# A chunked mLSTM with a gated network behind it: q and k transposed by TensorE in four tiles and scored in fp32, in place of scaled halves and DMA transposes

## The chip, the cores and the metric

The kernel runs on one core of a Trainium2 chip. The metric is the device time of one execution in microseconds (us). TensorE (PE) multiplies matrices, VectorE (DVE), ScalarE (ACT) and GpSimd (POOL) work on elements, SyncE (SP) issues most DMAs. PE's clock is granted in shares of full speed; the profile shows the share.

## The reference

Inputs: q, k, v and the output gate o, each (4 batches, 8 heads, 768 tokens, 40), two scalar gates per head and token, and three matrices of a network.

```
for t in range(S):
    m_new = np.maximum(f_gate[:, :, t] + m, i_gate[:, :, t])
    f_stab = np.exp(f_gate[:, :, t] + m - m_new)
    i_stab = np.exp(i_gate[:, :, t] - m_new)
    m = m_new
    C = f_stab * C + i_stab * einsum('bhd,bhe->bhde', vt, kt)
    n = f_stab * n + i_stab * kt
    h_tilde = einsum('bhde,bhe->bhd', C, qt)
    denom = np.maximum(np.abs(einsum('bhd,bhd->bh', n, qt)), 1.0)
    y[:, :, t] = sigmoid(o_gate[:, :, t]) * h_tilde / denom
# y as x (4, 768, 320):
gate = sigmoid(causal depthwise convolution of x with 5 taps)
return (gate * (x @ w_val)) @ w_out
```

All of it is fp32; the three matrices of the network come as 64-bit numbers, which the kernel turns into fp32 itself.

## The kernel before, in words

**Tiling.** The 768 tokens are cut into 6 steps `j` of 128 tokens, each step into two chunks `p` of 64. A unit of work `u = 4 j + b` is a step and a batch: a pair of chunks, 8 heads each. A chunk is numbered `g = 2 u + p`, 48 in all. Inside a chunk the recurrence is written as attention: a matrix of 128 rows (64 keys of the chunk and, on the other 64 rows, the state carried in, of which 40 or 41 are used) by 64 queries, per head.

**The steps of a chunk.** `args` (L357): one bf16 matmul gives the exponents' arguments of 8 heads, psd; `expo` (L368, ACT) takes their exponential, dm. `scores` (L384) gives k times q for the keys and q itself for the state rows, pss. `probs` (L391, DVE) multiplies the two, pt. `keyw` (L403, POOL) weights the keys, kw. `heads` (L437, L439) is written by hand, alternating for each head a matmul of the output, ph, into one half of PE's columns with one of the new state, pc, into the other. `state_out` (L419, ACT) copies the state into the values' tile vc of the next chunk. For each pair follow `norm` (L448 to L452, DVE), `norm_o` (L457, POOL), `gate_o` (L462, DVE) and a transpose of the result, px (L471), whose copies feed the network.

**How scores are made.** q and k are loaded in their natural layout, tokens on partitions, into nat. For each batch the largest absolute value of a token is taken (`prep_max`, L288, ACT), a power of two is made of it by integer arithmetic (`prep_scale`, L293 to L300, DVE), and the scaled values are split into two fp16 halves and a copy of the first (`prep_hi`, L322, POOL; `prep_lo`, L327 and L336, DVE), side by side in a tile stk of 128 by 8 heads by 128. A DMA transpose of the whole tile (`prep_tr`, L347, SP) gives tq or tk with the 120 used columns on partitions; an fp16 matmul over these 120 sums the products of the halves. `probs` takes the scale of k out again, and the norm uses the scale of q, which is brought into the tokens' order by small matmuls (L309, L315, L316). A second set of DMAs copies k from nat into kp (L197), the natural layout with the state rows that `keyw` needs.

**The network.** Each step's 128 tokens of the four batches go through it about a step later: `conv0`, `conv` and `conv3` (L496, L502, L514), sigmoid (L522), `val` (L537, pf), products and their split into two parts (L542 to L551), `outp` (L563, po), stored by L568 and L572. The last step runs in two halves of two batches. In the first third, the matrices are loaded and converted on DVE, POOL and ACT (L581 to L623).

**Order.** Start-up is written out by hand. Behind it, every step is put on a list with a time in chunks (the table LAGS gives a lag for each step, some for single `j`), the list is sorted, and a scheduler orders each engine's instructions from that; SP keeps the list's order. Inside the marked blocks PE keeps the written order of its instructions, though others may come between. The psd, pss, px, pg, pf and po tiles share five PSUM buffers, ph has two, pc one.

Of the kernel before, what the change touches and what calls it, by code (L numbers as in the profile page):

```python
# [8 lines left out]
F32 = mybir.dt.float32  # L9
# [79 lines left out]
def tile_mlstm_gated_ffn(  # L89
# [26 lines left out]
    SB = 14  # L116
# [4 lines left out]
    R = B  # L121
    PB = P // B
# [32 lines left out]
    nat = [cst.tile([P, 2, BH, D], F32, name=f"nat{i}") for i in range(2)]  # L155
    kp = cst.tile([P, 2, BH, D], F32, name="kp")
# [16 lines left out]
    tk_ = [cst.tile([P, L + H * (P + L)], F16, name=f"tk{i}") for i in range(3)]  # L173
    cmp_ = [cst.tile([P, 2, B], F32, name=f"cmp{i}") for i in range(2)]
    sct = [cst.tile([P, B], F32, name=f"sct{i}") for i in range(2)]
    spg = cst.tile([P, PB, R], BF16, name="spg")
    sel_g = cst.tile([P, PB], F32, name="sel_g")
    sel_b = cst.tile([P, B], BF16, name="sel_b")
    scl = [cst.tile([P, 2, B], F32, name=f"scl{i}") for i in range(2)]
    amx = [cst.tile([P, 2, B], F32, name=f"amx{i}") for i in range(2)]  # L180
    stk = [cst.tile([P, 2, H, P], F16, name=f"stk{i}") for i in range(2)]


    def load_qk(j, x, b0, b1):
        ts = slice(j * P, (j + 1) * P)
        if x == 1 or j == 0:
            hs = slice(b0 * H, b1 * H)
            nc.sync.dma_start(nat[j % 2][:, x, hs], (qv, kv)[x][ts, hs])
            return
        dst = nat[j % 2][:, 0].rearrange("p (h r) d -> p h (r d)", r=R)  # L190
        for b in range(b0, b1):
            nc.sync.dma_start(dst[b * PB : (b + 1) * PB], q[b, :, ts].rearrange("h (g r) d -> g h (r d)", r=R))

    def load_k(j, p, i):
        hs = slice(i * BH // 2, (i + 1) * BH // 2)
        put = nc.scalar.copy if j == i == 0 else nc.vector.tensor_copy if j < T["kpe"] else nc.sync.dma_start
        put(kp[TOK[p] : TOK[p] + L, p, hs], nat[j % 2][p * L : (p + 1) * L, 1, hs])  # L197
# [80 lines left out]
    MASKE = 0x7F800000  # L278

    def part(j, x, i):  # L280
        src = nat[j % 2][:, x]
        if x == 0 and j > 0:
            return src.rearrange("p (h r) d -> p h r d", r=R)[:, :, i]
        return src[:, i * H : (i + 1) * H]

    def prep_max(j, i, x):
        junk = wk.tile([P, H, D], BF16, name=f"junk{j}_{i}_{x}", tag="junk", bufs=1)
        nc.scalar.activation(junk, part(j, x, i), AF.Abs, accum_out=amx[j % 2][:, x, i : i + 1])  # L288

    def prep_scale(j, xs, i0, i1):  # L290
        a, s = (t[j % 2][:, xs, i0:i1] for t in (amx, scl))
        c = cmp_[j % 2]
        nc.vector.tensor_scalar_max(a, a, 2.0**-100)  # L293
        nc.vector.tensor_scalar(a.bitcast(I32), a.bitcast(I32), MASKE, None, op0=ALU.bitwise_and)
        nc.vector.tensor_scalar(
            s.bitcast(I32), a.bitcast(I32), -1.0, float((SB + 254) << 23), op0=ALU.mult, op1=ALU.add
        )
        for p in range(2 if xs.stop == 2 else 0):
            h = slice(TOK[p], TOK[p] + L)
            nc.vector.tensor_scalar(  # L300
                c.bitcast(I32)[h, p, i0:i1],
                amx[j % 2].bitcast(I32)[p * L : (p + 1) * L, 1, i0:i1],
                float(-(SB << 23)),
                None,
                op0=ALU.add,
            )
# [626 lines left out]
```

## Time and profile before

| | |
|---|---|
| median of 3 runs | 294.26 us (293.21 to 295.13) |
| the profiled execution's own time | 294.18 us |
| its span, first to last instruction | 292.4 us |
| mean granted PE clock | 0.837 |
| busy PE, DVE, ACT, POOL | 207.6, 227.9, 155.4, 176.7 us |
| DMA: bytes, packets | 38.73 MB, 145897 |

Busy time of PE is the union of its matmuls, whose ends are modelled and which overlap in its pipeline; how fast matmuls follow each other is read from their starts, or from the chain of waits, in which a piece lasts until the next begins. A slice of the page is 7.3 us.

### The profile page before, as it was taken

The numbers are of one execution on the slowest core, as the hardware profiler recorded it, in microseconds if no ns is written. First come the engines' busy times: TensorE is split into PE (matmuls) and PEld (weight loads), VectorE is DVE, ScalarE is ACT, GpSimd is POOL, SyncE is SP. The second block draws the span as 40 slices with busy tenths as digits, with TensorE's granted clock in tenths as the row PEclk, the third lists the DMA queues.
The fourth block names the chain that finished last, engine by engine and source line by source line (L and its number), as shares of the span: only waits on it lengthen the run. The fifth ranks groups of instructions, "written<-read, shape, count | busy, mean of one in ns | idle before, by whom it ended". The sixth has DMA issues, their size and how long they took to land.

```text
span 292.4 us, 6704 instructions
## 1 busy us (share of the span) xinstructions
PE 207.6 (71%) x2411; PEld 165.9 (57%) x2411; DVE 227.9 (78%) x526; ACT 155.4 (53%) x354; POOL 176.7 (60%) x276
## 2 busy tenths in 40 slices
PE   0037437526649374798479989876989999999985
PEld 0015325325437263575468666765767877787984
DVE  7999968757588999988999756997539992794950
ACT  4276642373774932578552497822288456346262
POOL 7566426533749844978964655783439762855541
PEclk9999755556855776789759999795799999999999
DMA  7899799999999995399953999975999230011112
GB/s 138 150 148 197 105 204 162 189 153 163 186 174 230 203 143 106 57 190 206 155 85 74 110 214 192 193 67 96 192 225 150 84 83 2 0 45 48 45 47 90
DMA packets 145897, 38.73 MB, mean 132 GB/s; under 512 B 135176, under 2 KB 143752, under 8 KB 145864
## 3 DMA queue, kind: packets, MB, share of 16 engines
q1 hardware_dynamic: 143044, 37.76, 79.0%
q10 hardware_dynamic: 2820, 0.54, 1.3%
q8 instruction: 19, 0.31, 0.5%
q14 instruction: 14, 0.11, 0.1%
HBM read 17.87 MB, written 4.23 MB: 76 GB/s over the span
## 4 chain that ended last, share of the span: by engine, by line
DVE 24%; PE 22%; POOL 14%; DMA 14%; issue 13%; ACT 6%; SPq 5%; ACTq 0%; POOLq 0%; DVEq 0%
DVE sg L502 6%; PE po L563 5%; PE ph L437 5%; PE pf L537 4%; DMA tq<-stk 4%; DMA tk<-stk 3%; DVE stk L327 3%; POOL kw L403 3%; DVE stk L336 3%; DMA sg<-in_o_gate_dram 2%; PE pss L384 2%; PE pg L514 2%; DMA kp<-nat 2%; DVE pt L391 2%; POOL xl L487 2%
## 5 line engine op out<-in xcount | busy, mean ns | idle before, releaser
L437 PE MATMUL ph<-vc,pt 128*64 128x41 f32 (+1 forms) x768 | 69.8, 258 | 28.6 <-ACT vc L419 17.3
L437 PEld LDWEIGHTS ph<-vc,pt 128*64 128x64 f32 (+1 forms) x768 | 61.9, 167 | 41.0 <-ACT vc L419 20.0
L322 POOL TENSOR_SCALAR stk<-nat,scl 128x320 f16<-128x320 f32 x48 | 32.9, 689 | 40.5 <-DMA tk<-stk 17.9
L502 DVE SCALAR_TENSOR_TENSOR sg<-xc,cwt,sg 128x512 f32<-128x512 f32 (+1 forms) x56 | 50.6, 934 | 4.1 <-POOL sg L496 4.0
L439 PE MATMUL pc<-vc,kw 128*40 128x41 f32 (+1 forms) x704 | 51.5, 236 | 3.1 <-POOL kw L403 1.8
L384 PE MATMUL pss<-tq,tk 120*128 120x64 f16 x384 | 35.5, 270 | 21.5 <-DMA tq<-stk 6.4
L439 PEld LDWEIGHTS pc<-vc,kw 128*40 128x40 f32 (+1 forms) x704 | 45.8, 137 | 7.1 <-issue 3.1
L384 PEld LDWEIGHTS <-tk 120*128 120x128 f16 x384 | 28.8, 134 | 34.5 <-issue 19.0
L368 ACT ACTIVATE dm<-psd 128x512 f32<-128x512 f32 x48 | 28.6, 597 | 32.0 <-DVE pt L391 19.9
L403 POOL TENSOR_TENSOR kw<-kp,dm 128x320 f32<-128x320 f32 (+1 forms) x44 | 37.3, 850 | 9.2 <-DMA kp<-nat 3.1
L391 DVE SCALAR_TENSOR_TENSOR pt<-pss,cmp,dm 128x512 f32<-128x512 f32 x48 | 35.6, 741 | 8.0 <-PE ph L437 6.4
L357 PE MATMUL psd<-ra,la 120*128 120x512 bf16 x48 | 23.7, 494 | 23.8 <-DMA la<-gda 18.4
L327 DVE SCALAR_TENSOR_TENSOR stk<-nat,scl,stk 128x320 f16<-128x320 f32 x48 | 31.7, 660 | 10.7 <-POOL stk L322 10.6
L288 ACT ACTIVATE junk<-nat 128x320 bf16<-128x320 f32 x48 | 22.5, 470 | 22.6 <-DMA nat<-in_q_dram 11.6
L457 POOL TENSOR_TENSOR rs<-sg,den 128x320 f32<-128x320 f32 x24 | 19.4, 807 | 22.4 <-DVE den L452 12.0
L419 ACT COPY vc<-pc 40x328 f32<-40x328 f32 x44 | 18.7, 425 | 24.8 <-PE ph L437 17.7
L487 POOL TENSOR_TENSOR xl<-xc,xh 128x256 fp32r<-128x256 f32 x24 | 19.9, 829 | 16.2 <-ACT xc L480 16.0
L542 DVE TENSOR_TENSOR sg<-pf,sg 128x512 f32<-128x512 f32 (+3 forms) x21 | 12.6, 609 | 13.7 <-ACT sg L522 6.5
L551 POOL TENSOR_TENSOR zl<-sg,zh 128x512 fp32r<-128x512 f32 (+1 forms) x14 | 16.1, 1156 | 11.1 <-ACT zh L546 11.0
L336 DVE COPY stk<-stk 128x320 f16<-128x320 f16 x48 | 21.3, 445 | 0.0
L563 PE MATMUL po<-woh,zh 128*128 128x320 f32 x72 | 19.8, 332 | 0.0
L563 PE MATMUL po<-wol,zh 128*128 128x320 f32 x72 | 18.7, 312 | 0.0
(150 smaller groups left out, 443.4 us busy)
## 6 DMA issues: line engine op xcount, KB each, us to landing
nat<-in_q_dram SPq DMA_DIRECT2D x24, 160.0 KB, 4.0
vc<-in_v_dram SPq DMA_DIRECT2D x12, 320.0 KB, 5.6
sg<-in_o_gate_dram SPq DMA_DIRECT2D x6, 640.0 KB, 6.6
out_dram<-ob SPq DMA_DIRECT2D x24, 160.0 KB, 2.4
kp<-nat SPq DMA_DIRECT2D x22, 160.0 KB, 3.5
nat<-in_k_dram SPq DMA_DIRECT2D x10, 320.0 KB, 4.7
nat<-in_k_dram SPq DMA_DIRECT2D x4, 160.0 KB, 3.5
rawv<-in_moe_w_val_dram SPq DMA_DIRECT2D x4, 160.0 KB, 3.2
```

Of the source, the lines that this page charges most:

```text
L322: return nc.gpsimd.tensor_scalar(o, v, f, 1.0, op0=ALU.mult, op1=ALU.mult)
L327: nc.vector.scalar_tensor_tensor(t[:, :, lo : lo + D], part(j, x, i), scl[j % 2][:, x, i : i + 1], t[:, :, 0:D], op0=ALU.mult, op1=ALU.sub ...
L336: return put(t[:, :, dup : dup + D], t[:, :, 0:D])
L368: nc.scalar.activation(dm, psd_[g], AF.Exp)
L384: nc.tensor.matmul(o, tk[h], tq[:, h], start=True, stop=True)
L391: nc.vector.scalar_tensor_tensor(pt, pss_[g], cmp_[j % 2][:, p, b : b + 1], dmt[g], op0=ALU.mult, op1=ALU.mult)
L403: (nc.vector if turn("on_dve_kw", b) else nc.gpsimd).tensor_mul(kw[0:n], kp[0:n, p, b * H : (b + 1) * H], dmt[g][0:n, :, L - 1 : L].to_bro ...
L437: nc.tensor.matmul(pht[u][p * L : (p + 1) * L, h], ptt[g][0:n, h], mv, start=True, stop=True)
L439: nc.tensor.matmul(pc[n0 : n0 + D, h], kwt[g][0:n, h], mv, start=True, stop=True)
L487: (nc.vector if turn("on_dve_xl", b) else nc.gpsimd).tensor_sub(xlb[j % 2][:, :, b], xb[:, :, b, 4:], xhb[j % 2].bitcast(F32)[:, :, b])
L502: nc.vector.scalar_tensor_tensor(o, xc[j % 2][:, c, b0:b1, t : t + P], cwt[:, c, t : t + 1], o, op0=ALU.mult, op1=ALU.add)
L563: nc.tensor.matmul(pf, z, w, start=(i == 0), stop=(i == len(mm) - 1))
```

## The change

q and k are no longer scaled, split and transposed by DMA. k is loaded straight from DRAM into kp, which now has two buffers, and q into nat, which holds q alone. For each pair `tr` (L276 of the changed kernel) transposes q and k on TensorE: fp32 matmuls of 64 tokens by 64 or 40 columns against a 64 by 64 identity. Two heads and the two chunks make four tiles of a quarter of the array each: the chunk chooses the row half, the head of a pair the column half. The result is two PSUM tiles pT per pair, one per chunk, with the even heads' 40 columns on the lower partitions and the odd heads' on the upper. `tr_out` (L287) copies them into SBUF, the first on ACT, the second on DVE (in the first step both on ACT). `scores` (L303, L307) then makes both chunks of a pair at once in fp32: 16 matmuls over 40 rows, again in quarter tiles, and 4 of 256 columns that carry q to the state rows through the identity; the results lie in two PSUM tiles pss, one for even and one for odd heads. `probs` (L337) becomes two multiplications per chunk, without a scale. The norm uses the constant 1. pT and pss come from the same five PSUM buffers as before. The scaling steps, their constants and the q scale's small matmuls are gone. Start-up is written anew: the first four pairs are transposed there, the first pair of chunks is scored there, the constants for the other steps are copied there, and the second spread of the gates goes out on SP. The table LAGS is as before; the transposes of a pair stand 4.7 chunks ahead of it, the loads of a step 11.6 and 7.6 chunks ahead. The copies of the identity into kp, four now, moved from ACT to POOL.

```
-    nat = [cst.tile([P, 2, BH, D], F32, name=f"nat{i}") for i in range(2)]
-    kp = cst.tile([P, 2, BH, D], F32, name="kp")
+    nat = [cst.tile([P, BH, D], F32, name=f"nat{i}") for i in range(2)]
+    kp = [cst.tile([P, 2, BH, D], F32, name=f"kp{i}") for i in range(2)]
...
+    def load_k(j, p, b0, b1):
+        hs = slice(b0 * H, b1 * H)
+        c = slice(j * P + p * L, j * P + (p + 1) * L)
+        nc.sync.dma_start(kp[j % 2][TOK[p] : TOK[p] + L, p, hs], kv[c, hs])
...
-    def prep_hi(j, i, x):
...
-        return nc.gpsimd.tensor_scalar(o, v, f, 1.0, op0=ALU.mult, op1=ALU.mult)
...
-        nc.sync.dma_start_transpose(t, stk[i % 2][:, x].rearrange("p h n -> p (h n)"))
...
+    def tr(u):
+        j, b = divmod(u, B)
+        pT = [ps_s.tile([P, 2, H // 2, L], F32, name=f"pT{u}_{r}", tag="big") for r in range(2)]
+        kf = kp[j % 2].rearrange("p x n d -> p (x n d)")
+        qf = nat[j % 2].rearrange("p n d -> p (n d)")
+        with tc.manual_schedule(engines={mybir.EngineType.PE}):
+            for h in range(0, H, 2):
+                for x in range(2):
+                    for r in range(2):
+                        rows = slice(r * L, (r + 1) * L)
+                        for i, m in ((0, L), (1, D)):
+                            c = (b * H + h + i) * D + (x * (1 - r)) * BH * D
+                            nc.tensor.matmul(
+                                pT[r][i * L : i * L + m, x, h // 2],
+                                (qf, kf)[x][rows, c : c + m],
+                                ident[rows, rows],
+                                start=True,
+                                stop=True,
+                            )
+        qk_ps[u] = pT
+
+    def tr_out(u, r):
+        t = wk.tile([P, 2, H // 2, L], F32, name=f"qk{u}_{r}", tag=f"qk{r}", bufs=4)
+        (nc.scalar.copy if r == 0 or u < B else nc.vector.tensor_copy)(t[0:NT], qk_ps[u][r][0:NT])
+        qk_[u, r] = t
...
+    def scores(u):
+        eo = [ps_s.tile([P, 2, H // 2, L], F32, name=f"pss{u}_{i}", tag="big") for i in range(2)]
+        q = [qk_[u, p][:, 0] for p in range(2)]
+        k = [qk_[u, 1 - p][:, 1] for p in range(2)]
+        rows = [slice(i * L, i * L + D) for i in range(2)]
+
+        with tc.manual_schedule(engines={mybir.EngineType.PE}):
+            for h in range(H // 2):
+                for p in range(2):
+                    for i, r in enumerate(rows):
+                        o = eo[i][TOK[p] : TOK[p] + L, p, h]
+                        nc.tensor.matmul(o, k[p][r, h], q[p][r, h], start=True, stop=True)
+            for p in range(2):
+                for i, r in enumerate(rows):
+                    o = eo[i][STA[p] : STA[p] + L, p]
+                    nc.tensor.matmul(o, ident[r, i * L : (i + 1) * L], q[p][r], start=True, stop=True)
...
-        nc.vector.scalar_tensor_tensor(
-            pt, pss_[g], cmp_[j % 2][:, p, b : b + 1], dmt[g], op0=ALU.mult, op1=ALU.mult
-        )
+        po, do = (t.rearrange("k (h i) l -> k i h l", i=2) for t in (pt, dmt[g]))
+        for i in range(2):
+            nc.vector.tensor_mul(po[:, i], pss_[u][i][:, p], do[:, i])
...
+            at(t - 4.7, tr, u)
+            for r in range(2):
+                at(t - 4.4, tr_out, u, r)
+        if u > 0:
+            at(t + lag("scores", j), scores, u)
```

PE in the kernel before, one pair of the third step, where nothing of the network lies between (names: psd the arguments, tk and tq the transposed halves, pss the scores, ph and pc the heads, px the result's transpose):

```order
L357 MATMUL psd_1457<-ra,la 128x512
L384 LDWEIGHTS tk_100
L384 MATMUL pss_1469<-tq_986,tk_100 128x4x16
...
L437 MATMUL ph_1283<-vc_85,pt_1312 64x41
L439 MATMUL pc_1355<-vc_85,kw_1213 40x41
...
L357 MATMUL psd_1516<-ra,la 128x512
L384 MATMUL pss_1522<-tq_986,tk_100 128x4x16
...
L437 MATMUL ph_1418<-vc_84,pt_1384 64x41
L439 MATMUL pc_1419<-vc_84,kw_1259 40x41
...
L471 MATMUL px_1533<-ident,x_1506 128x128 x2
```

Each chunk has its arguments, its eight scores and its eight heads in turn. PE in the changed kernel, a pair where the second step ends (nat holds q, kp holds k, pT the transposes of one chunk, qk their copies; pss_0 belongs to the even heads, pss_1 to the odd):

```order
L317 MATMUL psd_1545<-ra,la 128x512
L303 MATMUL pss_0_1559<-qk_0_1374,qk_1_1376 64x64
L303 MATMUL pss_1_1560<-qk_0_1374,qk_1_1376 64x64
...
L307 MATMUL pss_0_1559<-qk_0_1374,ident 64x256
...
L381 MATMUL ph_1518<-vc_86,pt_1542 64x41
L383 MATMUL pc_1588<-vc_86,kw_1417 40x41
...
L317 MATMUL psd_1619<-ra,la 128x512
L415 MATMUL px_1634<-ident,x_1609 128x128 x2
L276 MATMUL pT_0_1639<-ident,nat_81 64x64
L276 MATMUL pT_0_1639<-ident,nat_81 40x64
L381 MATMUL ph_1677<-vc_85,pt_1616 64x41
L276 MATMUL pT_1_1640<-ident,nat_81 64x64
```

The scores of both chunks stand together, and 32 transposes of a later pair come in, with the first head of the next pair among them. DVE in the kernel before, in the third step (stk the fp16 halves, pt the probabilities):

```order
L327 SCALAR_TENSOR_TENSOR stk_115<-nat_81,scl_110,stk_115 128x8x40
L336 COPY stk_115<-stk_115 128x8x40
L300 TENSOR_SCALAR cmp_104<-amx_113 64x2
L391 SCALAR_TENSOR_TENSOR pt_1384<-pss_1333,cmp_103,dm_1243 128x512
L327 SCALAR_TENSOR_TENSOR stk_114<-nat_82,scl_111,stk_114 128x8x40
L336 COPY stk_114<-stk_114 128x8x40
```

DVE in the changed kernel, a pair where the second step ends (qk_1 the second transposed tile, den the norm, x the result):

```order
L287 COPY qk_1_1549<-pT_1_1482 104x512
L337 TENSOR_TENSOR pt_1616<-pss_0_1559,dm_1451 128x4x64
L337 TENSOR_TENSOR pt_1616<-pss_1_1560,dm_1451 128x4x64
L392 TENSOR_SCALAR den_1614<-ph_1518 128x8
L337 TENSOR_TENSOR pt_1711<-pss_0_1559,dm_1552 128x4x64
L337 TENSOR_TENSOR pt_1711<-pss_1_1560,dm_1552 128x4x64
L394 TENSOR_TENSOR den_1614<-ph_1518,den_1614 128x8
L396 RECIPROCAL den_1614<-den_1614 128x8
L406 TENSOR_TENSOR x_1944<-ph_1518,rs_1709 128x320
```

The halves, copies and scale arithmetic are gone from DVE; one copy of a transposed tile and two half-size multiplications per chunk stand in their place.

More of the change, by code (lines that the diff above doesn't have):

```diff
@@ L172, in tile_mlstm_gated_ffn, with load_q @@
     cwt = cst.tile([P, 3, 5], F32, name="cwt")
[L173 to L197, printed above, removed]
+    def load_q(j, b0, b1):
+        hs = slice(b0 * H, b1 * H)
+        nc.sync.dma_start(nat[j % 2][:, hs], qv[j * P : (j + 1) * P, hs])
+    def load_k(j, p, b0, b1):
+        hs = slice(b0 * H, b1 * H)
+        c = slice(j * P + p * L, j * P + (p + 1) * L)
+        nc.sync.dma_start(kp[j % 2][TOK[p] : TOK[p] + L, p, hs], kv[c, hs])
     def load_v(j, p):
@@ L275, in spread_in @@
             )
[L278 to L296, printed above, removed]
-        )
[L298 to L306, printed above, removed]
@@ L308, in scale_mul @@
-    def scale_mul(j):
-        nc.vector.tensor_mul(
-            spg, sel_g[:, :, None].to_broadcast([P, PB, R]), scl[j % 2][:, 0, None, :].to_broadcast([P, PB, R])
-        )
-    def scale_out(j):
-        pq = ps_s.tile([P, B], F32, name=f"pq{j}", tag="big")
-        nc.tensor.matmul(pq, spg.rearrange("p g r -> p (g r)"), sel_b, start=True, stop=True)
-        nc.vector.tensor_copy(sct[j % 2], pq)
-    def prep_hi(j, i, x):
-        o, v, f = stk[i % 2][:, x, :, 0:D], part(j, x, i), scl[j % 2][:, x, i : i + 1]
-        if j > 0 and turn("on_act_hi", 2 * i + x):
-            return nc.scalar.activation(o, v, AF.Copy, scale=f)
-        return nc.gpsimd.tensor_scalar(o, v, f, 1.0, op0=ALU.mult, op1=ALU.mult)
@@ L761, in tile_mlstm_gated_ffn @@
-        nc.vector.tensor_copy(sct[0], scl[0][:, 0])
-        run(rest)
-        spread_out(1, nc.scalar.dma_start)
-        for i in range(2):
-            load_qk(1, 1, 2 * i, 2 * i + 2)
-        nc.gpsimd.memset(gt[L:P, 2], 0.0)
-        i4 = ident.rearrange("p (b g) -> p b g", b=B)
-        with nc.allow_low_precision("one of each sum is 1, the others 0"):
-            nc.vector.tensor_reduce(sel_b, i4, axis=AX.X, op=ALU.add)
-        nc.vector.tensor_reduce(sel_g, i4.rearrange("p b g -> p g b"), axis=AX.X, op=ALU.add)
@@ L772, in consts1 @@
-    def consts1():
-        for j in range(1, NJ):
-            yield nc.vector.tensor_copy(ra[:, :, j], tr)
-            yield nc.vector.tensor_copy(la[:, :, j], tl)
+        for g in range(2):
+            args(g)
+        scores(0)
+        for g in range(2):
+            expo(g)
+            keyw(g)
+        for _ in range(6):
+            next(rest)
+        for g in range(2):
+            probs(g)
+        sig_o(0)
+        run(rest)
+        spread_out(1, nc.sync.dma_start)
+        *_, last_dve = consts1()
@@ L777, in consts2 @@
+        load_q(1, 0, B)
+        for p in range(2):
+            load_k(1, p, 0, 2)
+        spread_in(1, nc.sync.dma_start)
+        for p in range(2):
+            load_k(1, p, 2, 4)
     def consts2():
@@ L779, in consts2 @@
             yield vc_const(1, p)
+        for p in range(2):
+            yield kp_const(1, p)
+        nc.gpsimd.memset(gt[L:P, 2], 0.0)
         nc.gpsimd.memset(xc[0][:, :, :, 0:4], 0.0)
```

191 lines of the change are left out of this document (45 added, 146 removed).

## The prediction

> **What bounds the kernel now.** I read the page's busy shares and slices first, then one row per stage, then the chain of waits for prices at full clock.
>
> ```profile
> PE 207.6 (71%) x2411; PEld 165.9 (57%) x2411; DVE 227.9 (78%) x526; ACT 155.4 (53%) x354; POOL 176.7 (60%) x276
> PE   0037437526649374798479989876989999999985
> DVE  7999968757588999988999756997539992794950
> PEclk9999755556855776789759999795799999999999
> DMA  7899799999999995399953999975999230011112
> ```
>
> No engine is full throughout. DVE (VectorE) is nearest; the DMA engines stay at 9 tenths for most of the first 30 slices, while PE (TensorE) gets half its clock in slices 6 to 13. So I cut the span into start-up (A), the first eight pairs of chunks (B, little gated-network work), the other sixteen (C), and the tail behind the last heads (D), by the starts of the heads' matmuls. The columns are PE, weight loads, DVE, ACT (ScalarE) and POOL (GpSimd) busy, then clock, DMA share, GB/s.
>
> ```profile
> 0.00:22.90 22.90, 2.32 (x21) 1.37 (x21) 20.30 (x59) 10.77 (x24) 14.36 (x35) 1.00 0.91 150
> 22.90:115.40 92.50, 50.76 (x694) 39.99 (x694) 76.14 (x195) 47.99 (x116) 53.78 (x88) 0.65 1.10 171
> 115.40:258.30 142.90, 124.87 (x1496) 98.05 (x1496) 112.78 (x238) 81.42 (x180) 94.36 (x136) 0.89 0.76 122
> 258.30:292.40 34.10, 29.62 (x203) 26.51 (x202) 18.70 (x38) 15.21 (x36) 14.16 (x18) 1.00 0.17 59
> 240.00:265.00 25.00, 25.00 (x231) 19.77 (x231) 16.69 (x32) 12.71 (x28) 14.46 (x21) 1.00 0.08 27
> PE pss L384 <- DMA tq<-stk: 6.4, 1, 6.4
> POOL stk L322 <- DMA tk<-stk: 10.4, 6, 3.9
> ```
>
> B is slow, 92.5/8 = 11.6 us a pair, with DMA over-full (1.10), PE at 0.65 clock, and waits on the DMA transposes (the last two rows, waits of B). C takes 8.9 us a pair; there PE and DVE are both about four fifths used. The row 240 to 265 shows that PE can be kept full, at full clock, once its work is there.
>
> **Prices of PE's work at full clock**, from the chain of waits (start, us, what):
>
> ```profile
> 242.71 0.46 PE pss L384 x8
> 243.18 0.22 PE psd L357
> 243.39 1.06 PE ph L437 x16
> 249.63 0.33 PE px L471 x3
> 240.35 2.36 PE pg L514 x10
> 244.45 2.06 PE pf L537 x8
> 229.95 2.56 PE po L563 x16
> 281.40 2.81 PE pf L537 x24
> ```
>
> A pair of chunks needs today two heads (2.12), two exponents' arguments (0.44), two scores (0.92), one px (0.33): 3.81 us. The gated network of one 128-token step needs 2.36 + 3 x 2.06 + 2 x 2.56 = 13.7; four steps lie in C. So C needs 16 x 3.81 + 4 x 13.7 = 116 of 142.9 us: 81%.
>
> **What the change adds on PE.** Per pair 32 fp32 matmuls of transposes and 20 of scores, each run as two passes (the 8 ph of a chunk are the x16 above), in place of 16 fp16 ones. No row shows a 64-row tile. The nearest are the heads: 64 columns of weights, 41 columns streamed, ph in one column half and pc in the other.
>
> ```profile
> 243.39:244.45 1.06, 1.06 (x18) 1.00 0.00 0
> 246.51:247.56 1.05, 1.05 (x33) 1.00 0.00 0
> 239.16 0.23 PE L437 MATMUL ph<-vc,pt 128*64 128x41 f32 x1
> 239.17 0.22 PE L439 MATMUL pc<-vc,kw 128*40 128x41 f32 x1
> ```
>
> Sixteen ph alone take 1.06 us, sixteen ph with sixteen pc 1.05 (the first two rows are windows with PE's busy time and records): the second column half rides free. Without the 0.1 that a change of tiling takes, below, it is 0.06 us a pass in each half. Transposes have 64 passes. Two wide, as these rows are, that is 32 x 0.06 = 1.9 us; four wide 0.96; one by one 3.8. Scores have 32 passes of the same width (0.96 two wide, 0.48 four wide) and 8 that stream 256 columns, where 2.81/24 = 0.12 holds (0.48 or 0.24): 1.44 or 0.72. The row halves are untested here, so I stand between: 1.5 and 1.1, an estimate. A pc starts 0.01 us behind a ph, so I set no floor under the distance of two starts. The Trainium skill's TensorE: Matmul & The Clock Gate, section "Wait — 56ns, not 53.3ns?", has one: about 25 ns from start to start however small the matmul. The 0.01 disagrees for neighbours in different column halves; by that floor transposes cost 64 x 25 = 1.6 and scores 0.8 + 0.48 = 1.3, the forecast below some 5 us more.
>
> Changing between tilings costs too:
>
> ```profile
> 238.97 0.17 PE ph L437
> 239.18 0.03 PE ph L437
> 240.03 0.32 PE psd L357
> ```
>
> The first ph behind the scores takes 0.17, a later one 0.03; the psd behind the heads 0.32 against 0.22: about 0.1 at each change. In PE's order a pair has four changes before and eight or nine after (arguments, scores, heads, arguments with px, transposes, the next heads in the midst of these): +0.5 us.
>
> Together 3.81 - 0.92 + 1.5 + 1.1 + 0.5 = 6.0 us a pair, +2.2.
>
> **What it takes off the others.**
>
> ```profile
> L327 DVE SCALAR_TENSOR_TENSOR stk<-nat,scl,stk 128x320 f16<-128x320 f32 x22 | 13.9, 633 | 3.4 <-POOL stk L322 3.4
> L336 DVE COPY stk<-stk 128x320 f16<-128x320 f16 x22 | 8.6, 392 | 0.0
> L300 DVE TENSOR_SCALAR cmp<-amx 64x2 int32<-64x2 int32 (+1 forms) x14 | 5.0, 360 | 0.3
> L391 DVE SCALAR_TENSOR_TENSOR pt<-pss,cmp,dm 128x512 f32<-128x512 f32 x48 | 35.6, 741 | 8.0 <-PE ph L437 6.4
> L542 DVE TENSOR_TENSOR sg<-pf,sg 128x256 f32<-128x256 f32 x4 | 1.6, 422 | 2.7 <-ACT sg L522 2.5 <-PE pf L537 0.2
> L368 ACT ACTIVATE dm<-psd 128x512 f32<-128x512 f32 x48 | 28.6, 597 | 32.0 <-DVE pt L391 19.9
> L322 POOL TENSOR_SCALAR stk<-nat,scl 128x320 f16<-128x320 f32 x48 | 32.9, 689 | 40.5 <-DMA tk<-stk 17.9
> L288 ACT ACTIVATE junk<-nat 128x320 bf16<-128x320 f32 x48 | 22.5, 470 | 22.6 <-DMA nat<-in_q_dram 11.6
> nat<-in_q_dram SPq DMA_DIRECT2D x24, 160.0 KB, 4.0
> ```
>
> The first three rows are of B alone, the others of the whole run. In B DVE loses 13.9 + 8.6 of halves and copies, and of the scale arithmetic the 5.0 and about as much again in its smaller neighbours. Over the run it gains 20 copies of a transposed tile out of PSUM, at 0.6 (the L368 size) to 0.74 each some 13 us, and its probabilities become 96 half-size operations, 2 x 0.42 for 0.74: +5. ACT loses 22.5 and gains 28 copies of 0.6: -6. POOL loses 32.9. All three then lie below PE in C. SP (SyncE) loses 48 transposes and 22 copies of k; the loads left wait only for free buffers and are queued about three chunks ahead of the first transpose of them, so I cost them at nothing. If that cover fails, a load is exposed at a step's start, the 4.0 of the last row in each of 5 steps, 20 us.
>
> **Stage by stage.** A: PE still waits for the gates' round trip through DRAM.
>
> ```profile
> 18.41 0.59 PE L357 MATMUL psd<-ra,la 120*128 120x512 bf16 x1 [18.41 <-DMA la<-gda]
> ```
>
> The gates' DMAs now stand on ACT behind two copies of transposes, but the transposes of q and k that slowed the landing are gone; the first probabilities no longer stand behind stk work, while six long gate scans now run ahead of them in DVE's idle time. POOL gets the constants of both buffers ahead of its first kw. Between +2 and -3; I take 21.5.
> B: DVE 76.1 - 22.5 - 10 + 4 (4 of the 20 copies, 16 of the 48 probabilities) = 48; PE 8 x 6.0 = 48 at full clock. Neither can be full, since behind the first probabilities DVE's order has the rest of the gates and ten copies of constants, for which PE waits. At the 81% that C has today: 60, against 92.5.
> C: 16 x 6.0 + 4 x 13.7 = 151. PE now has the most work by far, so between the 81% of today and the 100% of 240 to 265 I take 92%: 164, against 142.9.
> D: the same work in the same order, 34.1.
> Sum 21.5 + 60 + 164 + 34.1 = 279.6, and 1.8 outside the span (294.18 profiled against 292.4): 281. The profiled run lies 0.1 under the median 294.26, so it needs no correction. The gain of DMA and DVE in B (32) is mostly paid back by PE in C (21).
>
> **Rivals.** 1. *Only two tiles at a time.* Transposes 1.9, scores 1.44: +0.74 a pair, 16 x 0.74/0.92 = 13 in C and up to 3 in B: 296, no change. For it: only column halves are shown. Against: the row halves use other rows and other PSUM tiles.
> 2. *Slower: row halves take turns.* PE's order changes the row half every second matmul in the transposes and every one in the scores, 32 times a pair. If each change costs the 0.1 us above, a pair costs 0.74 + 3.2 more: C +69, B (8 x 9.9)/0.92 = 86, +26: 376; it decides from a hundredth of a microsecond a change on, since without any it is rival 1. Against it: ph and pc take turns within 0.01 us. The Trainium skill's TensorEngine Tiling (Array Packing), section Key Properties, holds that a change of mode drains the engine, a change of tile alone does not; no row here shows a row half.
> 3. *Slower: the clock stays at half.*
>
> ```profile
> 68.22 1.04 PE pss L384 x8
> 201.00:204.40 3.40, 3.40 (x51) 2.94 (x49) 2.04 (x5) 1.22 (x4) 2.59 (x5) 0.50 0.62 111
> 207.80:211.20 3.40, 3.40 (x39) 2.05 (x35) 1.78 (x4) 1.03 (x2) 1.19 (x3) 1.00 0.76 168
> ```
>
> At half clock scores take 1.04 for 0.46, so B would need 8 x 12 = 96 instead of 60: 317. Against it: a full window at 0.50, nearly all heads, has the clock at 1.00 some 3 us on. For it: quarter-array tiles may not count as full work. The same TensorE page, section "Part 4: PE-mode transpose", says that transposes in that mode do not bring the clock up; here they are plain matmuls with the identity, which no run shows yet.
> 4. *Four tiles in full.* Transposes 0.96, scores 0.72: -0.92 a pair, 16 us less in C, 2 in B: 263.
> That the DMA transposes stay is excluded: SP's order has none.
>
> **Numbers.** About 1% is what a measurement here can tell from no change: 291.3 to 297.2. Forecast 0.55, rival 1 0.17, rival 2 0.05, rival 3 0.10, rival 4 0.13. The forecast's own spread (C at 81% would be 186, thus 303; exposed loads) puts 0.04 of it within 1% and 0.04 above; rival 1 is 0.03 faster, 0.07 same, 0.07 slower. Faster: 0.47 + 0.03 + 0.13 = 0.63; same 0.11; slower 0.04 + 0.07 + 0.05 + 0.10 = 0.26. The range runs from rival 4 with PE at 96% (C 16 x 5.1 + 54.8 = 136, /0.96 = 142: 257) to 312, past rival 1 and the 81% case; beyond lie rival 2 and most of rival 3.
>
> **What would show it.** Right: B near 60 us at a clock above 0.85, PE above 90% busy in C, DMA share well under 0.7, transposes of a pair inside 1.2 to 1.8 us, no wait on a load over 2 us. Wrong: transposes near 1.9 and scores 1.44 (rival 1) or 3 us and more (rival 2), half clock in B with PE full (rival 3), DVE or the five PSUM buffers ending PE's waits in C (nine tiles a pair now pass through them instead of seven), or a long DMA wait at a step's start.

## The result, and the profile after

The changed kernel takes 322.6 us (median of 4, 320.9 to 329.6) against 293.8 for the kernel before on the same chip: a ratio of 1.095 (95% interval 1.086 to 1.105). The forecast was 281. Its profiled execution took 320.9 us, 318.6 of it the span. Four of the profiles below, marked * (the first without conversion, conversions later, late and pinned, loads by need without the hop), are of executions 1.5 to 3% longer than the faster ones of the same kernel, so their B may be some us too long and their C is not given.

The same cut into stages as in the prediction, with B cut once more at the first head of pair 4 (columns as there: PE, weight loads, DVE, ACT, POOL busy, clock, DMA share, GB/s):

```profile
0.00:23.70 23.70, 12.45 (x329) 9.38 (x330) 20.28 (x26) 7.96 (x12) 19.71 (x39) 0.77 0.79 113
23.70:73.00 49.30, 30.19 (x536) 22.71 (x536) 24.50 (x68) 18.04 (x32) 17.71 (x31) 0.59 0.75 105
73.00:128.70 55.70, 34.70 (x693) 26.65 (x693) 28.91 (x68) 21.04 (x45) 23.89 (x35) 0.60 0.46 66
128.70:284.40 155.70, 140.91 (x2765) 108.06 (x2763) 83.36 (x193) 79.94 (x159) 70.96 (x109) 0.96 0.37 59
284.40:318.60 34.20, 29.75 (x203) 26.44 (x202) 17.74 (x37) 15.19 (x36) 15.27 (x19) 1.00 0.17 58
```

The two halves of B in the kernel before:

```profile
22.90:71.90 49.00, 25.54 (x346) 20.41 (x346) 38.29 (x113) 22.73 (x60) 22.88 (x36) 0.62 1.12 167
71.90:115.40 43.50, 25.22 (x351) 19.59 (x350) 37.85 (x84) 25.27 (x57) 30.91 (x52) 0.69 1.09 175
```

| stage | before | forecast | after |
|---|---|---|---|
| A | 22.9 | 21.5 | 23.7 |
| B (halves) | 92.5 (49.0 + 43.5) | 60 | 105.0 (49.3 + 55.7) |
| C | 142.9 | 164 | 155.7 |
| D | 34.1 | 34.1 | 34.2 |

C and D come out as forecast or better. The miss is B, 45 us over its forecast (C gives 8 back): its first half didn't move although DVE lost a third of its work and the DMA share fell from 1.12 to 0.75, and its second half grew by 12 us with no engine busy for more than 63% of it.

**PE.** From the chain of waits in C (start, us, what), then two windows of C:

```profile
128.97 1.07 PE pT L276 x57
131.31 0.62 PE pss L303 x32
131.93 0.43 PE pss L307 x8
```

```profile
129.00:130.00 1.00, 1.00 (x60) 0.90 (x60) 1.00 0.00 0
130.99:136.59 5.60, 5.60 (x174) 4.44 (x174) 3.33 (x11) 3.22 (x8) 3.02 (x5) 1.00 1.01 164
```

The first window holds transposes alone: 60 records in a microsecond, 17 ns each at full clock. One after the other they would take the 0.06 us a pass of the prediction's rows, so all four tiles run at once. The second goes from one pair's arguments to the next pair's: PE full, 5.60 us, for which 6.0 was forecast. Only 14 of the 16 pairs have transposes in C (895 records there, 64 a pair), so it needs 14 x 5.60 + 2 x 4.53 (without the 1.07 of transposes) + 54.8 = 142 of 155.7 us, 91%.

**B.** The waits of B that tell most (us in total, times, longest):

```profile
PE ph L381 <- ACT vc L363: 15.7, 2, 8.1
PE ph L381 <- DVE pt L337: 15.2, 4, 8.3
DVE ca_vo L525 <- DMA rawvo<-in_moe_w_out_dram: 8.5, 1, 8.5
DVE ca_c L525 <- DMA rawc<-in_moe_conv_w_dram: 7.9, 1, 7.9
DVE ca_v L525 <- DMA rawv<-in_moe_w_val_dram: 7.2, 1, 7.2
DVE ca_o L525 <- DMA rawo<-in_moe_w_out_dram: 5.9, 1, 5.9
```

raw are the network's matrices as they come, in 64 bits; ca is the first operation of their conversion. DVE stands 29.5 us before them, with probabilities (pt) queued behind, for which PE waits. In the kernel before this view has one such row:

```profile
DVE ca_v L581 <- DMA rawv<-in_moe_w_val_dram: 2.5, 1, 2.5
```

One case in order of time, on SP and then on DVE:

```profile
58.41 0.53 SPq L174 DMA_DIRECT2D nat<-in_q_dram  x1
74.39 0.37 SPq L186 DMA_DIRECT2D sg<-in_o_gate_dram  x1
74.86 3.70 SPq L179 DMA_DIRECT2D kp<-in_k_dram  x2
78.66 1.95 SPq L548 DMA_DIRECT2D rawvo<-in_moe_w_val_dram  x1
```

```profile
75.23 0.69 DVE L287 COPY qk<-pT 104x512 f32<-104x512 f32 x1
84.38 0.33 DVE L525 TENSOR_SCALAR ca_vo<-rawvo 128x320 int32<-128x320 int32 x1 [8.45 <-DMA rawvo<-in_moe_w_out_dram]
```

In SP's own waits this is the longest (rs is the norm times the output gate, which GpSimd makes):

```profile
SPq L186 <- POOL rs L401: 15.4, 1, 15.4
```

SP stands from 59 to 74.4 at step 2's output gate, whose buffer step 0 still uses; the load of rawvo waits behind it. The planner had counted on rawvo, so its conversion stands next in DVE's queue, and DVE idles 8.5 us.

### The profile page after: what moved, and what is told of

The parts are those of the page before. It is cut to its first block, busy times and chain, and to the rows that moved or that the text cites. A ratio compares the mean times of both kernels' runs of the same rounds, so it can differ in the third digit from the quotient of the medians.

```text
span 318.6 us, 10472 instructions
## 1 busy us (share of the span) xinstructions
PE 248.0 (78%) x4518; PEld 193.2 (61%) x4518; DVE 174.8 (55%) x388; ACT 142.2 (45%) x282; POOL 147.5 (46%) x230
## 4 chain that ended last, share of the span: by engine, by line
PE 44%; DVE 17%; SPq 8%; ACT 7%; POOL 7%; DMA 4%; issue 3%; ACTq 0%; DVEq 0%; POOLq 0%
DVE sg L446 10%; PE ph L381 9%; PE po L507 8%; PE pT L276 6%; PE pg L458 4%; PE pf L481 3%; PE pss L303 3%; PE pc L383 3%; PE psd L317 3%; ACT sg L466 2%; PE pss L307 2%; PE px L415 2%; SPq L548 2%; SPq L179 2%; POOL zl L495 2%
## 5 line engine op out<-in xcount | busy, mean ns | idle before, releaser
L381 PE MATMUL ph<-vc,pt 104*64 104x41 f32 (+1 forms) x768 | 71.1, 257 | 37.6 <-DVE pt L337 21.4
L381 PEld LDWEIGHTS ph<-vc,pt 104*64 104x64 f32 (+1 forms) x768 | 61.8, 165 | 51.3 <-DVE pt L337 23.1
L276 PE MATMUL pT<-ident,nat 64*64 64x64 f32 (+1 forms) x768 | 39.5, 265 | 12.8 <-DVE sg L486 7.3
L337 DVE TENSOR_TENSOR pt<-pss,dm 128x256 f32<-128x256 f32 x96 | 35.8, 414 | 18.7 <-PE pss L307 17.4
L276 PEld LDWEIGHTS pT<-ident,nat 64*64 64x64 f32 (+1 forms) x768 | 32.6, 159 | 18.9 <-DVE sg L486 7.7
L276 PE MATMUL pT<-ident,kp 64*40 64x64 f32 (+1 forms) x768 | 35.3, 263 | 4.5 <-DMA kp<-in_k_dram 4.5
L276 PEld LDWEIGHTS pT<-ident,kp 64*64 64x64 f32 (+1 forms) x768 | 30.8, 160 | 5.0 <-DMA kp<-in_k_dram 5.0
L287 ACT COPY qk<-pT 104x512 f32<-104x512 f32 x28 | 15.9, 586 | 25.3 <-PE pT L276 19.9
L317 PE MATMUL psd<-ra,la 120*128 120x512 bf16 x48 | 21.5, 452 | 6.2 <-ACT qk L287 2.2
L495 POOL TENSOR_TENSOR zl<-sg,zh 128x512 fp32r<-128x512 f32 (+1 forms) x14 | 16.3, 1167 | 21.5 <-ACT zh L490 21.5
L406 DVE TENSOR_TENSOR x<-ph,rs 128x320 f32<-128x320 f32 x24 | 11.8, 490 | 24.1 <-POOL rs L401 13.5
L490 ACT CAST zh<-sg 128x512 fp32r<-128x512 f32 (+3 forms) x21 | 11.6, 560 | 22.7 <-DVE sg L486 22.6
L303 PEld LDWEIGHTS pss<-qk,qk 40*64 40x64 f32 x768 | 16.1, 152 | 8.7 <-issue 7.4
```

The source lines that it names most:

```text
L276: nc.tensor.matmul(pT[r][i * L : i * L + m, x, h // 2], (qf, kf)[x][rows, c : c + m], ident[rows, rows], start=True, stop=True,)
L303: nc.tensor.matmul(o, k[p][r, h], q[p][r, h], start=True, stop=True)
L317: nc.tensor.matmul(psd, la[:, p, j, b], ra[:, :, j], start=True, stop=True,)
L337: nc.vector.tensor_mul(po[:, i], pss_[u][i][:, p], do[:, i])
L381: nc.tensor.matmul(pht[u][p * L : (p + 1) * L, h], ptt[g][0:n, h], mv, start=True, stop=True)
L495: (nc.vector if turn("on_dve_zl", m) else nc.gpsimd).tensor_sub(o, gate_at(0, n, m, b0, b1), ff[0].bitcast(F32)[0:n, m, b0:b1])
```

## Experiments

The theory after the result: **late data**. The kernel's order is planned; an engine that reaches an instruction whose load SP issues late stands with all its queue behind it. Rivals: the new tilings cost PE more than C shows; the half clock itself holds B; and, later, a **serial chain**, by which the latency of a group sets B whatever is loaded when.

The complete kernels by stage (from the starts of the heads in the profiles), and the ratio to the kernel before; those that leave something out follow below:

| kernel | B, first half | second | C | ratio (95%) |
|---|---|---|---|---|
| before | 49.0 | 43.5 | 142.9 | 1 |
| changed | 49.3 | 55.7 | 155.7 | 1.095 (1.086 to 1.105) |
| weights early | 49.7 | 37.9 | 155.6 | 1.037 (1.033 to 1.042) |
| transposes twice | 57.5 | 59.1 | 175.3 | 1.204 (1.198 to 1.209) |
| DMA transposes back | 50.6 | 38.4 | 159.3 | 1.057 (1.052 to 1.061) |
| weights early, gates moved | 53.3 | 37.5 | 155.6 | 1.047 (1.040 to 1.054) |
| gates moved | 51.5 | 55.4 | 156.2 | 1.107 (1.101 to 1.114) |
| copies on ScalarE | 52.3 | 36.8 | 158.7 | 1.046 (1.041 to 1.051) |
| all loads early | 55.3 | 32.4 | 156.7 | 1.033 (1.023 to 1.043) |
| gates loaded early | 53.7 | 46.8 | 156.2 | 1.082 (1.072 to 1.091) |
| loads by need | 46.5 | 30.3 | 159.6 | 1.008 (1.004 to 1.012) |
| conversions later * | 46.8 | 44.5 | | 1.044 (1.035 to 1.053) |
| late conversions, pinned * | 37.2 | 43.9 | | 1.005 (1.000 to 1.009) |
| pinned | 49.1 | 32.9 | 156.6 | 1.022 (1.015 to 1.029) |
| loads by need, no hop * | 47.8 | 33.4 | | 1.000 (0.996 to 1.003) |
| late conversions, pinned, no hop | 37.2 | 41.8 | 156.8 | 1.011 (1.005 to 1.016) |

### Weights early

```
-        raw = wt.tile(..., name=f"raw{nm}", tag="raw", bufs=2)
+        raw = wt.tile(..., name=f"raw{nm}", tag=f"raw{nm}")
...
         load_o(0)
+        load_weights()
```

> All raw weight loads (taps, the five blocks of 320 columns) get buffers of their own and are issued at start-up behind the first output gate's load, so that no conversion on VectorE waits for SP's queue. Late weights (my theory: in stage B VectorE stands 29.5 us behind raw weight loads that SP, held by loads that wait for buffers, issues late, and PE, ACT and POOL wait for VectorE): stage B falls from 105 to 75-85 us, its granted clock rises from 0.60 to over 0.75, C stays at 152-160, the time is 292-303 us. Tiling price (rival: PE itself is slower in B by the four tiles' mode changes and by fp32 scores): B stays at 100-108, time 316-325. Half clock as a cause (rival: the gate keeps PE at half speed in B whatever VectorE does): the waits of VectorE go, but B stays over 95 at a clock near 0.6, time 310-322.

B fell from 105.0 to 87.6, C stayed:

```profile
23.60:73.40 49.80, 31.44 (x535) 23.71 (x535) 33.97 (x87) 22.41 (x41) 27.25 (x40) 0.83 0.79 122
73.40:111.30 37.90, 27.61 (x695) 21.84 (x693) 20.09 (x49) 17.01 (x36) 16.18 (x26) 0.77 0.56 72
111.30:266.80 155.50, 140.71 (x2765) 108.03 (x2763) 83.40 (x194) 79.97 (x159) 70.83 (x109) 0.96 0.38 59
```

The 17 us came out of the second half alone, and the rows of DVE before raw are gone. Half of those 29.5 us (rawc and rawv, 15.1) lay in the first half, which gained nothing from it. Late weights are a cause, of 17 of the 45 us; B and the time (about 303.6) end just above the bounds expected. The second half's clock rose from 0.60 to 0.77 with it; the clock's records of this run begin at 49 us, and what has no record counts as full, so the first half's 0.83 says nothing.

### Transposes twice

```
-            for h in range(0, H, 2):
+            for h in [h for h in range(0, H, 2) for _ in range(2 if u >= B else 1)]:
```

> The transposes of pairs 4 to 23 are computed twice in place (same values): 64 more matmul records a pair, 1.07 us at full clock and 1.9 us at half. Late weights: PE has 40 us of idle time in B, so B's 6 or so pairs that hold transposes cost at most 5 us there; C is PE's, so it rises by 15 to 18 us over its 14-16 pairs; time 337-346. Tiling price, or half clock with PE as the bound of B: B rises too, by 8-12 us, time 346-360. If neither stage is bound by PE, less than 8 us in all.

```profile
23.60:140.30 116.70, 67.20 (x1611) 52.96 (x1611) 53.36 (x135) 39.62 (x76) 41.34 (x65) 0.68 0.52 76
140.30:315.60 175.30, 158.15 (x3662) 124.38 (x3660) 80.46 (x194) 80.02 (x159) 69.16 (x109) 0.93 0.33 53
```

C rose by 19.6, 1.4 us for each of its 14 pairs, so C is PE's. B rose by 11.7, where I had expected at most 5; this and the time, 352, are in the rivals' bounds. The 40 us in which PE idles in B were no cover. But PE's own work isn't what fills the 11.7: its busy time in B rose by 2.3 us alone (67.2 for 64.9, at a clock of 0.68 for 0.60), and the first half, with two pairs' transposes, rose by 8.2, the second, with four, by 3.4. DVE's stands before raw loads rose with it, from 29.5 to 35.7 us:

```profile
DVE ca_v L525 <- DMA rawv<-in_moe_w_val_dram: 9.8, 1, 9.8
DVE ca_c L525 <- DMA rawc<-in_moe_conv_w_dram: 9.3, 1, 9.3
DVE ca_vo L525 <- DMA rawvo<-in_moe_w_out_dram: 9.2, 1, 9.2
DVE ca_o L525 <- DMA rawo<-in_moe_w_out_dram: 7.4, 1, 7.4
```

That PE waits for the others and they for PE, so that what is added to one is added to all, is a reading of this that no run shows.

### Without conversion

The weights are constants; their loads and the conversion from 64 bits are left out.

> Leaves out the loads of the network's weights and taps and their conversion from 64 bits: the weights are constants set on POOL, the split into two fp32r halves stays. Late weights: the bound of what e1 can win, and VectorE's own work for the conversions goes too; B falls to 60-72, C as it was, time 278-293. Tiling price: B keeps over 95 us, time over 310. Half clock as a cause: B over 90 at a clock near 0.6, time over 305.

B is 84.5 (43.7 + 40.8) *, and one run took 303.3 us: no better than weights early. My bounds were missed by 10 us and more; something else holds B. ACT stood 13.2 us before the sigmoids of output gates.

### DMA transposes back

```
+            for x in range(2):
+                at(t - 5.2, dummy, x)
```

`dummy` is a DMA transpose of 128 x 1024 2-byte numbers on SP, two a pair.

> The kernel with the weights loaded early (e1) and, on top, two DMA transposes for each of pairs 4 to 23 (128 x 1024 halves of 2 bytes, as the kernel before issued, result unused), on SP's queue about 5 group times ahead of the pair. If the DMA transposes' traffic was what held stage B before, as the prediction had it: B rises by 12-25 us over e1's and the time by 12-30 us. If stage B was held by late weights in the kernel before too, the traffic alone costs 0-5 us over e1.

B's row:

```profile
24.50:113.60 89.10, 59.11 (x1227) 45.17 (x1227) 53.18 (x135) 39.46 (x76) 41.64 (x65) 0.67 0.93 139
```

The DMA share of B rises from about 0.69 to 0.93, and B by 1.4 us (the time by 2%, most of it in C). So this traffic hardly costs anything in the changed kernel. That it held the kernel before was my reading; the run speaks against it but doesn't settle it: the share stays under the 1.10 of before, and nothing waits for these transposes, where the kernel before waited for its own (the 6.4 and 10.4 us in the prediction).

### Three attempts at the output gates

With the weights early, the chain runs twice through the load of an output gate, before whose sigmoid ACT stands with the exponents behind it. The table's times for the gates' loads and one sigmoid were moved; then the same in the changed kernel alone; then, with both, a copy of transposes went from DVE to ACT, away from DVE's bursts of convolution taps.

```
-    "og1": 4.264   "og2": -0.141   "sig2": -0.871
+    "og1": 1.0     "og2": 3.0      "sig2": 3.0
```

> The kernel with the weights loaded early, and three numbers of the table on top: the second step's output gate is loaded 3.3 group times earlier, the third's 3.1 later (behind the loads that it held up), and the third's sigmoid 3.9 later. Output gates' loads (theory: what is left over the forecast in stage B is ScalarE standing before the sigmoids for loads that SP issues late, 5.9 + 4.9 us, with the exponents of the next groups queued behind): B falls from 87.7 to 75-82 us and the time from 301-307 to 291-299. Serial chain (rival: B goes by the latency of one group's chain through PE, ScalarE, VectorE and GpSimd, and another wait takes the place of these two): B stays at 84-89, time 299-307.

> The changed kernel with the same three numbers alone; the weights are loaded where they were. Blocked queue (theory: the weights come late because SP stands 15.4 us at the third output gate's load, which waits for GpSimd to have used the first): the blocks vo and o of the weights land 12-20 us earlier, and B falls from 105 to 84-94 us, time 300-312. Weights late by place (rival: it is their place behind the loads of q and k that makes them late, not the blocked load): B 98-106, time 314-324.

> As the kernel with both (weights early, gates moved), and the second copy of each pair's transposes out of PSUM goes from VectorE to ScalarE for the pairs 4 to 23 too. VectorE's bursts (theory: seven or eight convolution taps in a row, 6.4-7.2 us a step, stand ahead of that copy in VectorE's queue, and PE's scores wait for it): 2-3 us a step less, 8-14 us in all against the kernel with both. PE-bound (rival: in C PE is 90% busy and the bursts are covered): within 3 us of it, or slower by 2-6 where ScalarE's queue (exponents, state copies) takes the place.

All three went the rivals' way, in the first two with B 1 to 2 us above even the rivals' bounds. In the first, ACT's waits were not removed:

```profile
ACT sg L469 <- DMA sg<-in_o_gate_dram: 12.6, 2, 7.7
```

As I read it, the planner places the sigmoid on ACT where it thinks that the load has landed, whatever time the table gives it: step 1's load went out at 46.9 us (54.4 with the weights early alone), and ACT stood ready for its sigmoid at 48.0 (55.1). In the second the wait for rawvo went, and rawc's grew from 7.9 to 11.6 us: one late load takes the place of another. In the third nothing is gained from the bursts (1.046 for 1.047); C is PE's.

### All loads early, and gates alone

The output gates of steps 1 and 2 are loaded at the end of start-up, step 2's into a tile of its own; with the weights also there (in `load_weights`), and without.

```
+    og2 = cst.tile([P, BH, D], F32, name="og2")
...
             load_k(1, p, 2, 4)
+        load_weights()
```

> Weights and the output gates of steps 1 and 2 are all loaded at the end of start-up, behind the loads of step 1's q and k (so that the gates' spread isn't held up as in the run with the weights early); step 2's output gate gets a tile of its own, so that its load waits for nobody. Late loads (theory: stage B is the forecast's 60 plus the times in which VectorE or ScalarE stand in order before data that SP issues late; of these 10.7 us of output gates and 4-5 us of the spread are left in the run with the weights early): B falls from 87.7 to 68-77 us, the time from 301-307 to 283-296. Serial chain (rival: the two numbers moved in the run before brought nothing because another wait was just behind): B 82-88, time 299-307.

> The changed kernel with the output gates of steps 1 and 2 alone loaded at the end of start-up, step 2's into a tile of its own; weights where they were. SP then isn't held for 15 us at that load, and ScalarE not before the two sigmoids. Late loads: both parts of the cause count by themselves; B falls from 105 to 82-93, time 300-311. Weights alone (rival: VectorE's wait for the weights is the whole cause and the gates are hidden behind it): B 98-105, time 316-324.

The second half fell to 32.4, but the first rose to 55.3, so B stayed at 87.7, as the rival had it. The chain shows why: SP issues 16 loads in a row, 0.6 us and more each, from 41 to 55 us, and the last of them, an output gate, lands 7 us later. Gates alone brought 4.5 us of B, and that too is in the rival's bounds.

### Loads by need, and what is left

The same loads in the order of need: taps and the blocks v0 and v1 (`a`) go where SP waits for the gates' rest anyway, step 1's output gate, vo, o0, o1 and step 2's output gate (`b`) behind step 1's q and k. Two more kernels bound the rest. One leaves out the gates of steps 1 to 5 and their spread, the loads and conversion of the weights, and the output gates of steps 1 and 2 (constants in their place); the other the first of these alone.

```
         sig_o(0)
+        load_weights_a()
         run(rest)
         spread_out(1, nc.sync.dma_start)
...
             load_k(1, p, 2, 4)
+        load_weights_b()
```

> As the kernel with all loads early, in the order of need: taps and the first two weight blocks in the gap in which SP waits for the gates' rest, then the spread and step 1's q and k, then step 1's output gate, the other weights, step 2's output gate. Cut stage B at the heads of pair 4: the first half takes 49.2 us in the changed kernel, 49.8 with the weights early, 55.3 with all loads early (49.0 in the kernel before); the second half 55.8, 37.9 and 32.4 (43.5). Start-up leftovers (theory: the first half is set by what start-up leaves behind the first heads: rest of the gates, their spread, constants, loads and weights, each issue 0.6 us of SP): first half 43-50, second 32-38, time 290-301. Serial chain (rival: a group's latency sets the first half whatever is loaded when): first half 50-56, time 299-306.

> Leaves out: the gates of steps 1 to 5 and their spread (exponents of those steps go by constants), the loads and the conversion of the network's weights (constants), the loads and sigmoids of the output gates of steps 1 and 2 (constants). All else runs. Start-up leftovers: the first half of B, 49.2 us, falls to 22-33, and B as a whole to 52-68, near the forecast's 60. Serial chain: first half over 38, B over 70.

> As the kernel with the loads in order of need, and leaves out only the gates of steps 1 to 5 and their spread (their exponents go by constants). Start-up leftovers: VectorE is free 5 us earlier, SP doesn't wait for the spread, and step 1's arguments don't wait for it to land: first half 36-44. If the weights' conversion and the output gates alone hold the first half: 46-52.

Loads by need, B's halves:

```profile
23.70:70.20 46.50, 30.74 (x535) 22.71 (x535) 34.66 (x87) 23.69 (x42) 27.05 (x40) 0.85 1.04 158
70.20:100.50 30.30, 25.89 (x695) 20.01 (x693) 20.13 (x50) 13.00 (x33) 16.12 (x26) 0.89 0.39 49
```

Without the leftovers:

```profile
22.90:58.10 35.20, 30.48 (x536) 22.68 (x534) 15.91 (x44) 15.85 (x31) 23.26 (x39) 0.55 0.94 121
58.10:88.20 30.10, 26.11 (x696) 20.14 (x692) 20.14 (x50) 13.01 (x33) 16.28 (x26) 0.89 0.31 40
```

Without less work, B goes from 105.0 to 76.8, 25.4 us of it in the second half, and the time to the kernel before's plus 0.8%. Part of this may come from the added buffers, with which these loads wait for nobody; against all loads early, which has the same buffers, the order alone brings 10.9 us. The tilings are the same in all of these, so that rival is out. So is the serial chain as what sets the first half: it had at least 50 us for it here, and over 38 without the leftovers.

With everything left out B is 65.3 and the time 280.9. That this is the forecast's 281 is luck: its B was 5.3 too low and its C 7.4 too high. The first half is still 35, above my 33: PE is busy for 30.5 of it at a clock of 0.55. The 0.85 of loads by need's first half can't be set against that, since the clock's records begin there at 50 us. Its heads' matmuls (duration in ns: least, median, most) take 308 ns before that, as in the changed kernel in a stretch with 0.50 on record, and 230 later:

```profile
L386 PE MATMUL ph<-vc,pt x65: 307/308/328, 23.8 to 41.1; 128*64 128x41 f32 x33, 104*64 104x41 f32 x32
L386 PE MATMUL ph<-vc,pt x109: 230/230/252, 68.2 to 88.0; 104*64 104x41 f32 x61, 128*64 128x41 f32 x48
```

The third told nothing: 306 us, since ACT reached the sigmoid of step 1's output gate 13.5 us before its load had landed, with copies of the state behind it, for which PE's heads waited:

```profile
PE ph L386 <- ACT vc L368: 17.7, 2, 15.6
ACT sg L474 <- DMA sg<-in_o_gate_dram: 18.5, 2, 13.5
```

### Can the rest be hidden?

From loads by need: the conversions left out; those not yet needed held until group 9; the same with three sigmoids pinned behind the exponents of later groups; pinned alone; and the one subtraction of a conversion that POOL does (the hop) given to DVE, in loads by need and in late and pinned. The diff shows the hold, the pin and the hop.

```
+            with tc.issue_after(last[0]), tc.issue_after(pt_last[9]):
...
+        with tc.issue_after(dm_last[(3, 10, 13)[j]]):
...
-        nc.gpsimd.tensor_sub(r, x.bitcast(F32), r)
+        nc.vector.tensor_sub(r, x.bitcast(F32), r)
```

> The kernel with loads in order of need, leaving out the weights' loads and their conversion (constants in their place); the output gates and the gates' rest and spread stay. Conversions hold the first half: 35-40 us. Gates and spread hold it: 43-48.

> The kernel with loads in order of need; the weight blocks vo and o are loaded in SP's gap ahead of the spread, the two output gates last, and VectorE's conversion of vo and o is held until the probabilities of group 9 are done. Conversions hold the first half (theory): it falls from 46.5 to 38-43 us, the second rises from 30.3 to 30-34, the time is 285-292. Gates and spread hold it (rival): first half 45-48, time 293-298.

> The kernel with conversions later, and the sigmoids of the output gates of steps 0, 1 and 2 pinned on ScalarE behind the exponents of groups 3, 10 and 13. In-order waits (theory): without the stands of ScalarE before the gates (10.8 us of it on the chain of the run before, 5 us ahead of the second heads) and with half of the conversions out of the first half, the first half is 36-42 us, the second 30-34, the time 282-289, faster than both kernels. Serial chain (rival): first half over 45, time over 293.

> The kernel with loads in order of need, with the same three sigmoids pinned, conversions where they were. In-order waits: first half 46.5 falls by the 4-5 us before the second heads to 40-43, second 30-33, time 287-292. If conversions and not the gates are the rest: 43-47, time 291-296, and the run with late conversions is faster by 4 us or more.

> The kernel with loads in order of need, and the one subtraction of each weight block's conversion that GpSimd does (0.87 us, six blocks) goes to VectorE (0.34-0.5 us). Hop through GpSimd (theory): first half 46.5 falls to 40-44 us, time from 293.7-297 to 288-292, faster than both kernels. VectorE's own work (rival): first half 46-49, time 294-299.

> The kernel with late conversions and pinned sigmoids, and the same subtraction on VectorE. Hop through GpSimd: the first half stays at 36-38 us, the second falls from 44.0 to 34-40, time from 293-297 to 284-291. VectorE's own work: second half 43-46, time 293-298.

Without the conversions (39.8 + 29.9 in B; ratio 0.986, 0.978 to 0.994) B is 7.1 us shorter than loads by need, and 4.4 longer than without all leftovers: the conversions hold 6.7 of the 11.3 us by which the first half is too long, as expected. Late conversions missed both bounds for the time (ratio 1.044): ACT stood 15.3 us before output gates. Pinned, late ones brought the first half to 37.2, as expected, and lengthened the second to 43.9, which I had at 30 to 34; in all 1.005. Pinning alone cost time (1.022 for 1.008). Without the hop the time fell by 0.8%, with intervals that just meet, and missed the 288 to 292 expected. The last kernel's second half, 41.8, is in neither bound; it shows what took the gain:

```profile
23.80:61.00 37.20, 27.16 (x536) 20.29 (x535) 27.85 (x78) 19.11 (x35) 18.61 (x32) 0.93 1.00 155
61.00:102.80 41.80, 38.28 (x693) 29.38 (x693) 28.20 (x61) 21.02 (x41) 21.35 (x28) 0.53 0.64 76
```

The same 690 or so matmuls that keep PE busy for 25.9 us at a clock of 0.89 in loads by need take 38.3 of 41.8 here at 0.53. PE at half clock is nearly the bound there; why the clock fell, no run shows. (The first half's 0.93 again lacks records, up to 46 us.) No complete kernel of these beats both; the best, loads by need without the hop, equals the kernel before (1.000) and is 9% faster than the changed one.

## Why the prediction was wrong

**Right.** C: PE became the bound, 91% full (forecast 92%), 5.60 us a pair for 6.0; transposes 1.07 us for 1.5, scores 1.05 for 1.1. The gap to 164 is the transposes: their price, and their number. The sum counted them for 16 pairs in C and 8 in B, but they run 4.7 chunks ahead, so C has those of 14 pairs, B of 6 and start-up of 4. A and D were right to 2.2 and 0.1 us, DMA share in C 0.37.

**The step that failed** is B, "at the 81% that C has today: 60". It took a share of use from a stage where PE is fed and put it on one where it isn't: in the changed kernel PE is busy for 65 of 105 us, 62%. Where the loads came in time the share held: in the second half of loads by need PE is 85% busy. Three parts:

- "DMA over-full (1.10), PE at 0.65 clock" as what made B slow in the kernel before. Without the DMA transposes B's first half is as long as it was (49.3 for 49.0), and most of their traffic put back costs B 1.4 us. What the first half of the kernel before (49.0) stood for wasn't tried by itself; that two kernels with so different work take the same 49 there speaks for start-up's leftovers in both, and is only argued.
- "The loads left wait only for free buffers [...] so I cost them at nothing." The order has more loads than those of q and k: the weights stand behind the blocked output gate in SP's queue, and their conversion ahead of probabilities in DVE's. Issued earlier, they give back 17 us; with the output gates, in order of need, 28. The price that I gave for a failed cover, 20 us, was about right; its place (q and k at a step's start) wasn't, and I held the failure for unlikely.
- "Behind the first probabilities DVE's order has the rest of the gates and ten copies" was seen and folded into the 81%. Leaving out these gates, the conversions and two output gates brings B from 76.8 to 65.3: 11.5 us that the forecast had not, nearly all in the first half.

So 105.0 = 65.3 that are left without leftovers, + 11.5 of leftovers, + 28.2 of loads that came late or in the wrong order. The 5.3 of the 65.3 above the forecast are in the first half, where PE is 87% busy at a clock of 0.55 and the forecast took full clock; that the clock is their cause wasn't tried. How the 11.5 could be hidden stays open: five kernels moved them about, and the best of them won 0.8%.

**Rivals.** 1 and 2 are out: four tiles run at once and row halves take no turns. 4 had the price of the transposes nearly right (0.96; 1.07 measured), not that of the scores (0.72; 1.05 measured). 3 said 317 from half clock in B "with PE full": the clock was 0.60, but PE was busy for 65 of 105 us, so the waits for data come first, and 28 us went with the loads' places and buffers. Where waits are shortened the half clock comes near to being the bound (0.53, PE 92% busy), so rival 3 is out as the cause of the miss and not as a limit behind it. The floor of about 25 ns between starts that the Trainium skill gives (TensorE: Matmul & The Clock Gate, "Wait — 56ns, not 53.3ns?") doesn't hold for four quarter tiles: 17 ns by the window above.

## What to carry to other kernels

When an operation leaves, the stages around it don't shrink to the busiest engine's work: list what each in-order queue holds there, DMA issues of other parts too, and ask of each wait which load it counts on and what stands behind. Don't count idle time of an engine in such a stage as cover: the doubled transposes cost 11.7 us where PE had 40 to spare. An order that a planner made for one timing must be made again, loads first, for another; here that, with a buffer for each load, took 28 us off B and about 26 off the time, nearly what the change itself had cost.

## What I had not expected

Quarter-array fp32 tiles start 17 ns apart at full clock, and 28 at half, by a window of transposes in the kernel with the weights early:

```profile
87.20:88.90 1.70, 1.70 (x60) 1.60 (x57) 0.50 0.81 137
```

Plain matmuls with the identity don't hold the clock down: it is 0.96 in C, where they are a fifth of a pair's time. And the clock can stay at half for 44 us, even through 10 us in which PE is busy throughout; the same matmuls then keep PE busy 12 us longer. Two windows of the last kernel:

```profile
56.20:100.40 44.20, 35.93 (x650) 27.81 (x652) 29.07 (x60) 23.52 (x47) 23.27 (x31) 0.50 0.72 85
80.00:90.00 10.00, 10.00 (x181) 7.56 (x173) 6.10 (x13) 6.75 (x11) 5.66 (x8) 0.50 0.18 23
```

The Trainium skill's TensorE: Matmul & The Clock Gate, "A second HAM failure mode: psum-queue depth-cycling", tells of a clock that goes back and forth between half and full because PE idles for short spells between groups of matmuls. These windows don't show that back and forth, and no run here shows why the clock stays at half.
